# Retention and a mixture of experts in one kernel: another order of loads and operands in the opening, and weights fetched two rounds ahead at the switch of batches

## The chip, the cores and the metric

The kernel runs on one core of a Trainium2 chip. The metric is the device time of one execution in microseconds (us). Five engines work side by side, each through its own instructions in order: TensorE (PE, with its weight load PEld), VectorE (DVE), ScalarE (ACT), GpSimd (POOL) and SyncE (SP), which here only issues DMA transfers. They wait for each other by semaphores.

## The reference

Retention over q, k, v of 4 batches, 8 heads, 768 steps and 64 features, and its result as the input of four experts:

```python
for t in range(S):
    state = gamma[None, :, None, None] * state + np.einsum('bhd,bhe->bhde', k[:, :, t], v[:, :, t])
    y[:, :, t] = scale * np.einsum('bhd,bhde->bhe', q[:, :, t], state)
...
x = np.ascontiguousarray(attn_out.transpose(0, 2, 1, 3)).reshape(B * S, H * D)
...
p = domain_probs / (domain_probs.sum(-1, keepdims=True) + 1e-09)
for e in range(E):
    h = np.maximum(x @ w1[e], 0.0)
    out += p[:, e:e + 1] * (h @ w2[e])
```

x is 3072 x 512, w1 is 4 x 512 x 1024, w2 is 4 x 1024 x 512, all float32.

## The kernel before, in words

**Retention.** A batch is cut into 6 chunks of 128 steps. For each chunk `scores` (L131) multiplies q and k on PE and DVE applies the mask (`sp`, L142); `scale_v` (L125) scales v by powers of gamma on POOL; `state` (L144) adds k times v to the running state `yst` (DVE, L159), which `decay` (L161) has scaled down on POOL; `values` (L169) computes the cross term (q with the old state, L180) and the inner term (`sp` with v, L186) on PE, and DVE writes the result to `xr` (L195). Chunk c's values are issued after the scores of chunk c + 1.

**Experts.** Each batch passes 16 rounds, a round being 256 columns of one expert's hidden layer. The products are split in a Strassen-like way: seven pieces (numbered 1 to 7) of sums and differences of x and of w1 per round, in the order 1, 5, 6, 2, 7, 3, 4 (round 0: 1, 2, 5, 6, 7, 3, 4). Every operand exists as a high part, a copy to a rounded float (`x_hi`, `w1_hi`, `hi2`, on ACT), and a low part, the remainder (`x_lo`, `w1_lo`, `lo2`, a subtraction of two SBUF tiles on DVE or POOL). A piece (`p1`, L483) is then six matmuls into a PSUM bank. Some pieces are copied out by ACT (`u`, L414) and added by DVE to the next (L420). `hidden` (L427) makes the high and low part of the hidden values in batch 0; the second product (`p2`, L526) of round n - 1 is issued between the pieces of round n, and DVE adds it up in `acc` (L545).

x is combined chunk by chunk: `first_x(c, part)` (L325) makes, for chunk c, the operands 5 and 6 (part 0: DVE computes t1 and t2, ACT their high, DVE their low parts) or 7, 3 and 4 (part 1: two subtractions on POOL, then high and low parts). x's operands 1 and 2 need no combination. A piece needs its operand from all three chunks of the batch's first half, and that half is combined with the second half, so chunks 3 to 5 have to be there first.

`combine_w1` (four subtractions or additions of 128x256), `w1_hi`, `w1_lo` in two parts (128x768 as loaded, 128x1024 combined) make a round's w1 operands; `combine_w2` makes w2's second set in place, between `hi2`/`lo2` of the first (`w2h`, `w2l`) and of the second (`c2h`, `c2l`). In batch 0 all of them are stored to DRAM (`save_w1`, `save_w2`); the later batches fetch them from there, a piece at a time (`fetch_w1`, L310, into five buffers named `v`). From round 16 on `gated` (L449) makes the hidden operands (`b`, high `oh`, low `ol`), and puts each step in a list `soon` with the number of pieces that it waits; `pass_step` (L477) issues what is due. The output units (`unit`, L553) of rounds 16 and 17 begin in round 18.

**What sets the order.** The program is written out by hand: each engine gets its instructions in the order of the Python statements. `weights(n, k)` (L332) hangs the preparation of the next round's weights on the pieces of this one; the opening (L629 to L692) is a loop over the six chunks with such steps hung on chunk numbers. Transfers are issued by SP, and a few by ACT, in order; eight completion semaphores go round, so each waits until the one eight before it has landed. In the opening some chunks' q, k, v land in buffers that later hold weights, since those are free.

Of the kernel before, what the change touches and what calls it, by code (L numbers as in the profile page):

```python
# [24 lines left out]
NB0 = S // 128  # L25
# [25 lines left out]
def retention_moe(ctx: ExitStack, tc: tile.TileContext, qk, kv, w1, w2, probs, probt, cmask, cqs, cks, cys, out, out_t):  # L51
# [64 lines left out]
            (eng or nc.sync).dma_start(out=t, in_=qk[ci])  # L116
            raw_qk[ci] = t

    def load_kv(ci, pool=None, tag=None, eng=None):
        if ci < NCH:  # L120
            t = (pool or in_p).tile([128, 2, H, D], F32, tag=tag or "kv", name="kv", bufs=None if pool else 2)
            (eng or nc.sync).dma_start(out=t, in_=kv[ci])
            raw_kv[ci] = t

# [207 lines left out]
    def weights(n, k):  # L332

        m = n + 1
        if n == 0:
            if k == 0:
                first_x(2, 0)
                first_x(1, 1)
                first_x(2, 1)
                combine_w1(1, nc.gpsimd)  # L340
            elif k == 3:
                kept.pop("c11")()
                w1_hi(1, 0)
                w1_lo(1, 0, nc.vector)
                load_w1(2)
                w1_hi(1, 1)
                w1_lo(1, 1, nc.gpsimd)
            elif k == 4:
                save_w2(0, wt2, 0)
                combine_w2(0, nc.gpsimd)  # L350
            elif k == 5:
                hi2(0, wc2, "c2")
                save_w1(0)
            elif k == 6:
                lo2(0, wc2, nc.vector)
                load_w2(1)
                save_w1(1)
            return
        if k == 0:
            save_w2(n - 1, wc2, 4)  # L360
            if m < NRND:
                load_w1(m + 1)
                combine_w1(m, nc.gpsimd)
                w1_hi(m, 0)
        elif k == 1:
            hi2(n, wt2, "w2")
            if m < NRND:
                w1_lo(m, 0, nc.gpsimd)
        elif k == 2:
            lo2(n, wt2, nc.vector)  # L370
            if n == 2:
                gates()
        elif k == 3:
            save_w2(n, wt2, 0)
            combine_w2(n, nc.gpsimd)
            if m < NRND:
                w1_hi(m, 1)
        elif k == 4:
            hi2(n, wc2, "c2")
        elif k == 5:  # L380
            if m < NRND:
                w1_lo(m, 1, nc.gpsimd)
            lo2(n, wc2, nc.vector)
            load_w2(n + 1)
        elif k == 6 and m < NRND:
            save_w1(m)


    kept_g = keep_p.tile([NE, NTOK], F32, tag="kg", name="kg")

# [58 lines left out]
    def gated(n, key, src):  # L449

        f, j = key
        t = npool["b"].tile([128, HB], F32, tag="b", name="b")
        g = gate[n // RPE][:, HB * j:HB * j + HB]
        nc.vector.scalar_tensor_tensor(out=t, in0=src, scalar=0.0, in1=g, op0=ALU.max, op1=ALU.mult)  # L454
        hb[n, key] = t
        sub = lambda o, a, b: nc.gpsimd.tensor_tensor(out=o, in0=a, in1=b, op=ALU.subtract)  # L456
        if key in ((0, 0), (1, 1)):
            i = 1 if key == (0, 0) else 3
            soon.append((0, lambda: op_hi(n, i, t)))
            soon.append((1, lambda: op_lo(n, i)))  # L460
        elif key == (0, 1):
            b11, b22, b12 = hb[n, (0, 0)], hb[n, (1, 1)], t

            soon.append((1, lambda: (sub(b11, b12, b11), sub(b12, b22, b12), sub(b22, b22, b11))))
            soon.append((2, lambda: op_hi(n, 5, b11)))
            soon.append((2, lambda: op_lo(n, 5)))
            soon.append((3, lambda: (op_hi(n, 7, b12), op_hi(n, 6, b22))))
            soon.append((3, lambda: (op_lo(n, 7), op_lo(n, 6))))
        else:
            b22 = hb[n, (1, 1)]  # L470
            soon.append((1, lambda: op_hi(n, 2, t)))
            soon.append((2, lambda: op_lo(n, 2)))
            soon.append((3, lambda: sub(t, t, b22)))
            soon.append((4, lambda: op_hi(n, 4, t)))
            soon.append((5, lambda: op_lo(n, 4)))

    def pass_step():  # L477
        now = [f for t, f in soon if t == 0]
# [150 lines left out]
    with tc.manual_schedule():  # L629
        warm = u_p.tile([128, HB], F32, tag="u", name="warm", bufs=3)  # L630
        nc.vector.memset(warm, 0.0)
        load_qk(0)
        load_kv(0, eng=nc.scalar)
        nc.scalar.dma_start(out=ks, in_=cks)
        nc.scalar.dma_start(out=mask, in_=cmask)
        nc.scalar.dma_start(out=qs, in_=cqs)
        load_qk(1, v_p, "w2h")
        load_kv(1)
        nc.scalar.dma_start(out=ys, in_=cys)
        load_qk(2, v_p, "w2l")  # L640
        load_kv(2, w_p, "w1h")
        load_qk(3, w_p, "w1l")
        load_w1(0)
        nc.sync.dma_start(out=pr, in_=probs)
        nc.sync.dma_start(out=gr, in_=probt)
        load_w2(0)
        load_qk(4)
        load_kv(3)
        load_qk(5, v_p, "w2h")
        load_kv(5, v_p, "w2l")  # L650
        load_kv(4)
        load_w1(1)
        wps = ps_z.tile([128, 512], F32, tag="z", name="ps_w")
        for w in WARM:
            nc.tensor.matmul(wps[:, 0:w], lhsT=warm[:, 0:128], rhs=warm[:, 0:w], start=True, stop=True)
        for ci in range(NCHB):
            old = ci > 0
            scale_v(ci)
            scores(ci)
            if ci == 5:  # L660
                first_x(0, 1)
            if old:
                values(ci - 1, ci < NCHB - 1)
            else:
                state(ci)()
            if ci + 1 < NCHB:
                decay(ci + 1)
            if ci == 1:
                w1_hi(0, 0)
                combine_w1(0, nc.vector)  # L670
                w1_lo(0, 0, nc.vector)
            elif ci == 2:
                w1_hi(0, 1)
                w1_lo(0, 1, nc.vector)
                nc.vector.tensor_reduce(out=ptot, in_=pr, op=ALU.add, axis=mybir.AxisListType.X)
                nc.vector.tensor_scalar(out=ptot, in0=ptot, scalar1=1e-9, scalar2=None, op0=ALU.add)
                nc.vector.reciprocal(out=prec[:, :, 0], in_=ptot)
                nc.vector.tensor_tensor(out=pm, in0=pr, in1=prec.to_broadcast([128, NB0, NE]), op=ALU.mult)
# [12 lines left out]
        start[0] = False  # L691
        values(ci, False)  # L692

        steps = iter(())
        for n in range(NRND * B):
# [114 lines left out]
```

## Time and profile before

| | |
|---|---|
| median of 3 runs | 1091.43 us (1091.34 to 1093.07) |
| profiled execution, its own time | 1093.62 us |
| its span from first to last instruction | 1090.7 us |
| PE busy | 1050.8 us |
| DVE, ACT, POOL busy | 724.4, 378.3, 679.6 us |
| mean granted TensorE clock | 0.992 |

The profile is of one execution. Its page gives busy times, the chain of work that ended last and the costliest groups of instructions. Further views answer for a stretch of time: busy time by stretch with the granted clock, the list of who waited for whom, and a timeline of one engine, where a row has the start, the length, the engine, the line, the operation, out<-in and, in brackets, the idle time before it with its releaser. `L142` is line 142 of the kernel printed above.

### The profile page before, as it was taken

The page shows a single profiled execution, that of the slowest core. Times are in us where ns is not written, and L with a number is a line of the kernel's source. Part 1 is how long each engine was busy: PE and PEld are TensorE (multiplying, and loading weights), DVE is VectorE, ACT ScalarE, POOL GpSimd, SP SyncE. Part 2 cuts the span into 40 slices and gives each one's busy share as a digit, 9 for nine tenths or more (in the row PEclk, how much of TensorE's full clock was granted, in tenths as well). Part 3 has the DMA queues.
Part 4 walks back from the last instruction along what each step waited for, and adds up shares of the span by engine and source line. Part 5 has one row for each costly group of instructions (what it writes and reads, how often), then busy time and mean ns, then how long its engine had stood idle before and what let it go on. Part 6 is the DMA issues. An engine that isn't in the chain of part 4 may idle for free.

```text
span 1090.7 us, 18579 instructions
## 1 busy us (share of the span) xinstructions
PE 1050.8 (96%) x6696; PEld 993.4 (91%) x6696; DVE 724.4 (66%) x1214; ACT 378.3 (35%) x737; POOL 679.6 (62%) x645
## 2 busy tenths in 40 slices
PE   6689999999999999999999899999999899999996
PEld 5578888888878999999999899999999899999995
DVE  5857666676766476676688556667669546666665
ACT  2343433444443423223252432332233343333330
POOL 3566666666626656556579655656668865555557
PEclk9899999999999999999999999999999999999999
DMA  8479999999898888878786987877788788888875
GB/s 323 145 261 312 345 308 312 300 347 310 285 303 291 262 268 265 277 258 271 242 260 219 331 279 238 272 266 257 233 256 261 254 270 253 261 262 256 265 223 168
DMA packets 154603, 293.70 MB, mean 269 GB/s; under 512 B 12688, under 2 KB 77328, under 8 KB 154512
## 3 DMA queue, kind: packets, MB, share of 16 engines
q1 hardware_dynamic: 153792, 291.66, 81.9%
q8 instruction: 53, 0.87, 0.3%
q10 hardware_dynamic: 720, 0.86, 0.2%
q14 instruction: 38, 0.31, 0.1%
HBM read 223.22 MB, written 69.26 MB: 268 GB/s over the span
## 4 chain that ended last, share of the span: by engine, by line
PE 81%; DVE 7%; POOL 5%; DMA 3%; issue 2%; ACT 1%; SPq 0%; ACTq 0%; DVEq 0%; POOLq 0%
PE ps_u L563 28%; PE ps_x L502 22%; PE ps_o L537 11%; PE ps_z L502 11%; PE ps_y L502 5%; POOL b L456 2%; POOL sum L578 2%; PE ps_s L139 2%; PE ps_v L186 2%; DVE xl L240 2%; DVE ol L447 1%; POOL ol L447 1%; PE ps_v L180 1%; DMA w2r<-in_w 1%; DMA v<-k 1%
## 5 line engine op out<-in xcount | busy, mean ns | idle before, releaser
L563 PE MATMUL ps_u<-oh,v 128*128 128x384 f32 x1344 | 395.5, 336 | 8.5 <-DVE sum L420 8.5
L456 POOL TENSOR_TENSOR b<-b 128x384 f32<-128x384 f32 x192 | 206.7, 1076 | 179.0 <-DVE b L454 147.5
L563 PEld LDWEIGHTS ps_u<-oh,v 128*128 128x128 f32 x1344 | 247.8, 188 | 12.2 <-DVE sum L420 12.0
L447 POOL TENSOR_TENSOR ol<-b,oh 128x384 fp32r<-128x384 f32 x192 | 207.8, 1094 | 81.1 <-ACT oh L442 43.5
L420 DVE TENSOR_TENSOR sum<-ps_u,sum 128x384 f32<-128x384 f32 x294 | 161.7, 550 | 136.4 <-PE ps_u L563 129.0
L442 ACT ACTIVATE oh<-b 128x384 fp32r<-128x384 f32 x336 | 163.1, 520 | 214.5 <-POOL b L456 123.8
L502 PE MATMUL ps_x<-xh,v 128*128 128x384 f32 x768 | 227.2, 336 | 1.3 <-ACT u L414 1.3
L563 PE MATMUL ps_u<-ol,v 128*128 128x384 f32 x672 | 225.0, 335 | 1.3 <-POOL ol L447 1.3
L414 ACT ACTIVATE u<-ps_x 128x384 f32<-128x384 f32 x128 | 62.6, 489 | 238.5 <-PE ps_x L502 238.4
L502 PEld LDWEIGHTS ps_x<-xh,v 128*128 128x128 f32 x768 | 141.4, 188 | 3.4 <-ACT u L414 1.6
L447 DVE TENSOR_TENSOR ol<-b,oh 128x384 fp32r<-128x384 f32 x144 | 127.9, 888 | 22.2 <-ACT oh L442 22.1
L502 PE MATMUL ps_x<-xl,v 128*128 128x384 f32 x384 | 128.4, 334 | 0.0
L563 PEld LDWEIGHTS ps_u<-ol,v 128*128 128x128 f32 x672 | 126.3, 188 | 1.7 <-POOL ol L447 1.7
L502 PE MATMUL ps_z<-xh,v 128*128 128x384 f32 x384 | 115.0, 340 | 2.4 <-DMA v<-k 2.4
L545 DVE SCALAR_TENSOR_TENSOR acc<-ps_o,pm,acc 128x512 f32<-128x512 f32 x90 | 67.0, 745 | 54.9 <-PE ps_o L537 54.9
L537 PE MATMUL ps_o<-w2l,hh 128*128 128x512 f32 x192 | 76.6, 399 | 0.0
L537 PE MATMUL ps_o<-w2h,hh 128*128 128x512 f32 x192 | 76.5, 398 | 0.2
L537 PE MATMUL ps_o<-w2h,hl 128*128 128x512 f32 x192 | 76.5, 398 | 0.0
L502 PEld LDWEIGHTS ps_z<-xh,v 128*128 128x128 f32 x384 | 71.6, 190 | 3.8 <-DVE c2l L290 2.7
L502 PEld LDWEIGHTS ps_x<-xl,v 128*128 128x128 f32 x384 | 72.1, 188 | 0.1
L502 PE MATMUL ps_z<-xl,v 128*128 128x384 f32 x192 | 64.8, 338 | 0.0
L420 DVE TENSOR_TENSOR ps_y<-ps_y,u 128x384 f32<-128x384 f32 x64 | 36.0, 563 | 33.6 <-PE ps_y L502 33.6
(109 smaller groups left out, 1630.5 us busy)
## 6 DMA issues: line engine op xcount, KB each, us to landing
v<-k SPq DMA_DIRECT2D x336, 256.0 KB, 3.8
v<-k SPq DMA_DIRECT2D x168, 512.0 KB, 4.5
k<-w1h SPq DMA_DIRECT2D x16, 896.0 KB, 6.3
k<-w1l SPq DMA_DIRECT2D x16, 896.0 KB, 8.4
qk<-in_qk SPq DMA_DIRECT2D x24, 512.0 KB, 5.5
kv<-in_kv SPq DMA_DIRECT2D x23, 512.0 KB, 5.8
w1r<-in_w SPq DMA_DIRECT2D x16, 512.0 KB, 7.9
w2r<-in_w SPq DMA_DIRECT2D x16, 512.0 KB, 4.3
```

The source lines that it names most:

```text
L139: nc.tensor.matmul(ps[r][:, p, :], lhsT=a[rows, 1, p, :], rhs=a[rows, 0, p, :], start=True, stop=True)
L186: nc.tensor.matmul(ps[r][64 * k:64 * k + 64, half, :], lhsT=v[:, 1, h, :], rhs=sp[:, h, :], start=(c == 0 and half == 0), stop=True, skip_ ...
L240: eng.tensor_tensor(out=lo, in0=x_part(b, i, o), in1=hi.bitcast(F32), op=ALU.subtract)
L414: nc.scalar.activation(out=t, in_=ps, func=ACTF.Copy)
L420: nc.vector.tensor_tensor(out=o, in0=ps, in1=u, op=ALU.add)
L442: nc.scalar.activation(out=hi, in_=t, func=ACTF.Copy)
L447: eng.tensor_tensor(out=lo, in0=t, in1=hi.bitcast(F32), op=ALU.subtract)
L456: sub = lambda o, a, b: nc.gpsimd.tensor_tensor(out=o, in0=a, in1=b, op=ALU.subtract)
L502: nc.tensor.matmul(ps, lhsT=lhsT[:, cs], rhs=rhs[:, kt, :], start=(fresh and m == 0), stop=(m == 5), skip_group_check=True,)
L537: nc.tensor.matmul(ps, lhsT=a[:, ts], rhs=b[:, fs, :], start=(m == 0), stop=(m == 5))
L545: nc.vector.scalar_tensor_tensor(out=acc[nt], in0=ps, scalar=sc, in1=acc[nt], op0=ALU.mult, op1=ALU.add)
L563: nc.tensor.matmul(ps, lhsT=w[:, r, l, ds], rhs=o, start=(m == 0), stop=(m == 5))
```

## The change

- **Loads.** mask and ks become the first two of ACT's transfers, ahead of v and k of chunk 0; ys goes ahead of qs. On SP round 0's w1 goes ahead of chunk 3's q; chunk 3's and 4's k and v land in the buffers of `c2h` and `c2l` and so wait for no one; probs move to the end; round 2's w1 is loaded in the opening.
- **Scaling.** v of chunk c + 1 is scaled after the state of chunk c and ahead of the decay for c + 1; before, v of a chunk was scaled at the chunk's own start.
- **Operands.** Round 0's `combine_w1`, both `w1_lo`, `lo2` of w2 and `x_lo` of operand 1 move from DVE to POOL. The four steps that normalise probs move out of the loop into `first_gates`, at piece 2 of round 0. `first_x(0, 1)` moves from the last chunk to round 0; `first_x(1, 0)` moves behind the last values. `combine_w2(0)` moves from piece 4 to piece 2, ahead of `w1_lo(1, 1)` on POOL; `hi2`, `lo2` of the second set and the next load of w2 move one piece up.
- **Switch.** The first four pieces of round 16's w1 are fetched at the start of round 14 and no longer in round 15; in round 16 `gated` doubles every wait in `soon`.

```diff
@@ weights, n == 0
             if k == 0:
                 first_x(2, 0)
+                first_x(0, 1)
                 first_x(1, 1)
                 first_x(2, 1)
                 combine_w1(1, nc.gpsimd)
+            elif k == 2:
+                first_gates()
+                save_w2(0, wt2, 0)
+                combine_w2(0, nc.gpsimd)
             elif k == 3:
                 kept.pop("c11")()
                 w1_hi(1, 0)
                 w1_lo(1, 0, nc.vector)
-                load_w1(2)
                 w1_hi(1, 1)
                 w1_lo(1, 1, nc.gpsimd)
             elif k == 4:
-                save_w2(0, wt2, 0)
-                combine_w2(0, nc.gpsimd)
-            elif k == 5:
                 hi2(0, wc2, "c2")
                 save_w1(0)
-            elif k == 6:
+            elif k == 5:
                 lo2(0, wc2, nc.vector)
                 load_w2(1)
+            elif k == 6:
                 save_w1(1)
@@ gated
+        slow = 2 if n == NRND else 1
+        later = lambda w, what: soon.append((w * slow, what))
...
-            soon.append((0, lambda: op_hi(n, i, t)))
-            soon.append((1, lambda: op_lo(n, i)))
+            later(0, lambda: op_hi(n, i, t))
+            later(1, lambda: op_lo(n, i))
...
@@ the opening
+        nc.scalar.dma_start(out=mask, in_=cmask)
+        nc.scalar.dma_start(out=ks, in_=cks)
         load_qk(0)
         load_kv(0, eng=nc.scalar)
-        nc.scalar.dma_start(out=ks, in_=cks)
-        nc.scalar.dma_start(out=mask, in_=cmask)
+        nc.scalar.dma_start(out=ys, in_=cys)
         nc.scalar.dma_start(out=qs, in_=cqs)
         load_qk(1, v_p, "w2h")
         load_kv(1)
-        nc.scalar.dma_start(out=ys, in_=cys)
         load_qk(2, v_p, "w2l")
         load_kv(2, w_p, "w1h")
+        load_w1(0)
         load_qk(3, w_p, "w1l")
-        load_w1(0)
+        load_kv(3, v_p, "c2h", 1)
+        load_qk(4)
+        load_kv(4, v_p, "c2l", 1)
+        load_qk(5, v_p, "w2h")
+        load_kv(5, v_p, "w2l")
+        load_w2(0)
+        load_w1(1)
         nc.sync.dma_start(out=pr, in_=probs)
         nc.sync.dma_start(out=gr, in_=probt)
-        load_w2(0)
-        load_qk(4)
-        load_kv(3)
-        load_qk(5, v_p, "w2h")
-        load_kv(5, v_p, "w2l")
-        load_kv(4)
-        load_w1(1)
...
+        scale_v(0)
         for ci in range(NCHB):
             old = ci > 0
-            scale_v(ci)
             scores(ci)
             if ci == 5:
-                first_x(0, 1)
+                first_x(0, 0)
             if old:
                 values(ci - 1, ci < NCHB - 1)
             else:
                 state(ci)()
             if ci + 1 < NCHB:
+                scale_v(ci + 1)
                 decay(ci + 1)
             if ci == 1:
                 w1_hi(0, 0)
-                combine_w1(0, nc.vector)
-                w1_lo(0, 0, nc.vector)
+                combine_w1(0, nc.gpsimd)
             elif ci == 2:
                 w1_hi(0, 1)
-                w1_lo(0, 1, nc.vector)
...
+                w1_lo(0, 0, nc.gpsimd)
             elif ci == 3:
-                hi2(0, wt2, "w2")
-                lo2(0, wt2, nc.vector)
                 for i in (1, 2):
                     x_hi(0, i)
-                    x_lo(0, i)
+                w1_lo(0, 1, nc.gpsimd)
+                x_lo(0, 1, eng=nc.gpsimd)
             elif ci == 4:
-                first_x(0, 0)
+                x_lo(0, 2)
+                hi2(0, wt2, "w2")
+                load_w1(2)
                 load_qk(6)
                 load_kv(6)
-            elif ci == 5:
-                first_x(1, 0)
         start[0] = False
         values(ci, False)
+        first_x(1, 0)
+        lo2(0, wt2, nc.gpsimd)
@@ the rounds
-                fetch_w1(t + 4)
+                if t == 7 * (NRND - 2):
+                    for x in range(4):
+                        fetch_w1(7 * NRND + x)
+                if t >= 7 * NRND:
+                    fetch_w1(t + 4)
```

Two places in the order of the built programs. First POOL in the opening, from the scaling of v of chunk 2; `kv` is the tile whose half v is scaled, `yst_115` and `yst_116` the two state tiles, `s` the combined w1, `w1l` its low part. Before:

```order
L127 TENSOR_TENSOR kv<-kv,ks 128x512
L165 TENSOR_TENSOR yst_115<-yst_115,ys 128x256
L127 TENSOR_TENSOR kv<-kv,ks 128x512
L165 TENSOR_TENSOR yst_116<-yst_116,ys 128x256
L127 TENSOR_TENSOR kv<-kv,ks 128x512
L165 TENSOR_TENSOR yst_115<-yst_115,ys 128x256
L127 TENSOR_TENSOR kv<-kv,ks 128x512
L212 TENSOR_TENSOR xr<-xr 128x2x128
```

The same place now, from just behind the decay for chunk 2:

```order
L265 TENSOR_TENSOR s<-w1r 128x256
L266 TENSOR_TENSOR s<-s,w1r 128x256
L267 TENSOR_TENSOR s<-w1r,s 128x256
L268 TENSOR_TENSOR s<-w1r 128x256
L127 TENSOR_TENSOR kv<-kv,ks 128x512
L165 TENSOR_TENSOR yst_115<-yst_115,ys 128x256
L282 TENSOR_TENSOR w1l<-w1r,w1h 128x768
L127 TENSOR_TENSOR kv<-kv,ks 128x512
L165 TENSOR_TENSOR yst_116<-yst_116,ys 128x256
L282 TENSOR_TENSOR w1l<-s,w1h 128x1024
L240 TENSOR_TENSOR xl<-xr,xh 128x768
L127 TENSOR_TENSOR kv<-kv,ks 128x512
```

The scaling and decays of chunks 3 to 5 now have w1's four combinations, its two low parts and one low part of x between them; the last decay and w2's low part (128x1024) follow.

Then ACT at the switch, in round 17: `u` is a copied piece that PE's next piece in that bank waits for, `oh` a high part of hidden values. Before:

```order
L414 ACTIVATE u<-ps_x 128x384
L442 ACTIVATE oh<-b 128x384 x2
L414 ACTIVATE u<-ps_z 128x384
L442 ACTIVATE oh<-b 128x384 x2
L414 ACTIVATE u<-ps_x 128x384
L442 ACTIVATE oh<-b 128x384 x3
```

The same place now:

```order
L422 ACTIVATE u<-ps_x 128x384
L422 ACTIVATE u<-ps_z 128x384
L450 ACTIVATE oh<-b 128x384
L422 ACTIVATE u<-ps_x 128x384
L450 ACTIVATE oh<-b 128x384 x5
```

Three of the four `oh` that stood between round 17's first and third copy now stand behind the third.

More of the change, by code (lines that the diff above doesn't have):

```diff
@@ L117, in load_qk, with load_kv @@
             raw_qk[ci] = t
-    def load_kv(ci, pool=None, tag=None, eng=None):
+    def load_kv(ci, pool=None, tag=None, bufs=None, eng=None):
         if ci < NCH:
-            t = (pool or in_p).tile([128, 2, H, D], F32, tag=tag or "kv", name="kv", bufs=None if pool else 2)
+            t = (pool or in_p).tile([128, 2, H, D], F32, tag=tag or "kv", name="kv", bufs=bufs if pool else 2)
             (eng or nc.sync).dma_start(out=t, in_=kv[ci])
@@ L386, in weights, with first_gates @@
             save_w1(m)
+    def first_gates():
+        nc.vector.tensor_reduce(out=ptot, in_=pr, op=ALU.add, axis=mybir.AxisListType.X)
+        nc.vector.tensor_scalar(out=ptot, in0=ptot, scalar1=1e-9, scalar2=None, op0=ALU.add)
+        nc.vector.reciprocal(out=prec[:, :, 0], in_=ptot)
+        nc.vector.tensor_tensor(out=pm, in0=pr, in1=prec.to_broadcast([128, NB0, NE]), op=ALU.mult)
     kept_g = keep_p.tile([NE, NTOK], F32, tag="kg", name="kg")
@@ L458, in gated @@
             i = 1 if key == (0, 0) else 3
-            soon.append((0, lambda: op_hi(n, i, t)))
-            soon.append((1, lambda: op_lo(n, i)))
+            later(0, lambda: op_hi(n, i, t))
+            later(1, lambda: op_lo(n, i))
         elif key == (0, 1):
             b11, b22, b12 = hb[n, (0, 0)], hb[n, (1, 1)], t
[L464 to L468, printed above, removed]
+            later(1, lambda: (sub(b11, b12, b11), sub(b12, b22, b12), sub(b22, b22, b11)))
+            later(2, lambda: op_hi(n, 5, b11))
+            later(2, lambda: op_lo(n, 5))
+            later(3, lambda: (op_hi(n, 7, b12), op_hi(n, 6, b22)))
+            later(3, lambda: (op_lo(n, 7), op_lo(n, 6)))
         else:
             b22 = hb[n, (1, 1)]
[L471 to L475, printed above, removed]
+            later(1, lambda: op_hi(n, 2, t))
+            later(2, lambda: op_lo(n, 2))
+            later(3, lambda: sub(t, t, b22))
+            later(4, lambda: op_hi(n, 4, t))
+            later(5, lambda: op_lo(n, 4))
     def pass_step():
@@ L669, in retention_moe @@
                 w1_hi(0, 0)
-                combine_w1(0, nc.vector)
-                w1_lo(0, 0, nc.vector)
+                combine_w1(0, nc.gpsimd)
             elif ci == 2:
                 w1_hi(0, 1)
-                w1_lo(0, 1, nc.vector)
[L675 to L678, printed above, removed]
+                w1_lo(0, 0, nc.gpsimd)
             elif ci == 3:
-                hi2(0, wt2, "w2")
-                lo2(0, wt2, nc.vector)
                 for i in (1, 2):
                     x_hi(0, i)
-                    x_lo(0, i)
+                w1_lo(0, 1, nc.gpsimd)
+                x_lo(0, 1, eng=nc.gpsimd)
             elif ci == 4:
-                first_x(0, 0)
+                x_lo(0, 2)
+                hi2(0, wt2, "w2")
+                load_w1(2)
                 load_qk(6)
                 load_kv(6)
-            elif ci == 5:
-                first_x(1, 0)
         start[0] = False
         values(ci, False)
+        first_x(1, 0)
+        lo2(0, wt2, nc.gpsimd)
         steps = iter(())
```

## The prediction

> **What bounds the kernel now.** I read the page first: TensorE (PE) is busy for 96% of the span, so all there is to gain are the few places where it is not. The table by stretches shows where those are. Its columns are busy time of PE, weight load, DVE, ACT and POOL, then the granted TensorE clock, the DMA share and GB/s.
>
> ```profile
> PE 1050.8 (96%) x6696; PEld 993.4 (91%) x6696; DVE 724.4 (66%) x1214; ACT 378.3 (35%) x737; POOL 679.6 (62%) x645
> 10.00:20.00 10.00, 8.53 (x154) 6.90 (x156) 8.17 (x17) 2.85 (x3) 3.41 (x4) 1.00 1.03 397
> 20.00:30.00 10.00, 5.13 (x100) 4.22 (x98) 9.90 (x16) 1.58 (x2) 5.63 (x4) 1.00 0.67 238
> 30.00:40.00 10.00, 7.10 (x81) 5.66 (x78) 9.91 (x20) 2.81 (x7) 5.35 (x6) 0.76 1.00 351
> 40.00:50.00 10.00, 7.50 (x33) 6.30 (x32) 9.21 (x16) 5.83 (x14) 5.24 (x7) 0.90 0.00 0
> 60.00:70.00 10.00, 8.02 (x33) 6.74 (x32) 5.00 (x9) 3.58 (x6) 5.62 (x6) 0.83 0.96 324
> 300.00:400.00 100.00, 96.17 (x568) 90.21 (x567) 60.00 (x98) 40.28 (x83) 51.29 (x49) 0.98 0.87 287
> ```
>
> From 20 to 50 us DVE is full (9.9, 9.9 and 9.2 us of 10) and PE is not: there DVE sets the pace. The clock falls as well, to 0.76, 0.90 and 0.83. The next hole that the change reaches is at the switch from batch 0 to batch 1. The list of PE's waits for 0 to 80 us and for 290 to 345 us (total, times, longest) names who is late:
>
> ```profile
> PE ps_v L153 <- POOL kv L127: 6.0, 4, 2.7
> PE ps_x L502 <- ACT u L414: 4.1, 3, 2.0
> PE ps_v L180 <- DVE sp L142: 2.5, 1, 2.5
> PE ps_z L502 <- DMA v<-k: 2.4, 1, 2.4
> PE ps_x L502 <- ACT u L414: 1.3, 1, 1.3
> ```
>
> The largest entry, v scaled by POOL too late, looks like the gain of this change. It isn't the term to count: what matters is when PE last waits in the opening. Those rows (start, length, engine, line) are these:
>
> ```profile
> 47.63 0.55 DVE L420 TENSOR_TENSOR ps_y<-ps_y,u 128x384 f32<-128x384 f32 x1
> 53.66 0.44 PE L502 MATMUL ps_z<-xh,w1h 128*128 128x384 f32 x1 [0.35 <-DVE hl L435]
> 56.03 1.06 ACT L286 ACTIVATE c2h<-w2r 128x1024 fp32r<-128x1024 f32 x1 [3.02 <-POOL w2r L298]
> 59.44 4.00 DMA w2r<-in_w
> 64.49 0.48 ACT u L414
> 65.02 0.44 PE L502 MATMUL ps_x<-xh,w1h 128*128 128x384 f32 x1 [1.98 <-ACT u L414]
> ```
>
> ```profile
> 75.42 1.04 PE ps_x L502 x6
> 77.50 1.39 PE ps_o L537 x6
> ```
>
> The last two, from the chain that ended last, are a piece and an output of TensorE at full clock. Call 47.63 us C: DVE starts round 0's first addition of hidden values. Call 65.02 us T: PE starts round 1's fifth piece. After T it waits for nothing up to round 16, so whatever T moves, the end moves.
>
> **Loads and scaling, up to C.** In the new order mask and ks go first and v is scaled a chunk ahead. That takes away the first wait for ks and the four waits for kv, and I count it at nothing by itself, because the six chunks now queue behind POOL. POOL receives five jobs that DVE had. Rows: the landing of w1, then POOL's decay and scaling (alone, and beside DVE), one addition, and the two sizes of low parts:
>
> ```profile
> 8.38 6.77 DMA w1r<-in_w
> 11.15 0.61 POOL L165 TENSOR_TENSOR yst<-yst,ys 128x256 f32<-128x256 f32 x1 [1.97 <-DVE yst L158]
> 11.72 1.04 POOL L127 TENSOR_TENSOR kv<-kv,ks 128x512 f32<-128x512 f32 x1
> 25.63 1.46 POOL L165 TENSOR_TENSOR yst<-yst,ys 128x256 f32<-128x256 f32 x1 [2.38 <-DVE yst L159]
> 27.05 1.75 POOL L127 TENSOR_TENSOR kv<-kv,ks 128x512 f32<-128x512 f32 x1
> 56.76 0.72 POOL L266 TENSOR_TENSOR s<-s,w1r 128x256 f32<-128x256 f32 x1
> 59.94 1.84 POOL L282 TENSOR_TENSOR w1l<-w1r,w1h 128x768 fp32r<-128x768 f32 x1
> 69.04 2.40 POOL L282 TENSOR_TENSOR w1l<-s,w1h 128x1024 fp32r<-128x1024 f32 x1
> 31.16 1.09 PE L186 MATMUL ps_v<-sp,kv 128*64 128x128 f32 x16
> 36.64 1.97 PE L186 MATMUL ps_v<-sp,kv 128*64 128x128 f32 x16
> 38.54 0.69 PE L502 MATMUL ps_x<-xh,w1h 128*128 128x384 f32 x1
> ```
>
> w1 landed at 15.15 us; one load of 512 KB fewer is ahead of it, 1.3 us at the 397 GB/s of 10 to 20 us, so 13.8. From there POOL has, in order: four combinations (4 x 0.8 with the gaps, 3.2), scaling and decay three times (3 x 1.65, 5.0), w1l 1.84 and 2.40, and xl of 128x768, taken as the w1l of that size, 1.84. Sum 14.3: it ends at 28.1 if nothing disturbs it. With the three pairs at their long lengths (1.46 and 1.75) it is 32.8. The long ones stood beside DVE's additions of two SBUF tiles, of which five are left in this time, so I take a value nearer the short end, 29.5. The last decay is what PE's last cross term waits for, so the attention ends 0.7 and 1.09 us later, V = 31.3 (32.8 with the 1.97 of the half clock). Before, it ended at 38.6: seven us won.
>
> They are spent at once. Between V and C DVE had ten additions on 128x256 pieces; now it has seventeen, and then the gates' four small steps:
>
> ```profile
> 21.70 0.17 DVE L675 TENSOR_REDUCE ptot<-pr 128x6 f32<-128x24 f32 x1
> 22.54 0.76 DVE L678 TENSOR_TENSOR pm<-pr,prec 128x24 f32<-128x24 f32 x1
> 36.73 0.41 DVE L240 TENSOR_TENSOR xl<-t,xh 128x256 fp32r<-128x256 f32 x1
> 43.22 0.92 POOL L265 TENSOR_TENSOR s<-w1r 128x256 f32<-128x256 f32 x1
> 43.47 1.83 DVE L240 TENSOR_TENSOR xl<-xr,xh 128x256 fp32r<-128x256 f32 x2
> ```
>
> One takes 0.41 us alone and 0.92 while POOL works on such a piece, which itself takes 0.92 in place of 0.72. POOL, after w2's low part (29.5 + 2.40 = 31.9), has fourteen such pieces without a wait: six of x, four of w1, four of w2; 14 x 0.92 = 12.9, until 44.8. DVE starts at V + 0.7 = 32.0, does fourteen of its own in that time, three more alone (1.2, to 46.0) and the gates (21.70 to 23.30, 1.6): C = 47.6, where it was. Bounds: all seventeen alone gives 32.0 + 7.0 + 1.6 = 40.6; all contended from V = 35.8 gives 53.7. I take 47.6, because POOL's fourteen pieces are really there.
>
> [...]
>
> **From C to T.** DVE, ACT and PE go hand to hand from C to 53.66, and the order there is kept: 6.0 us again. After it round 0's w2 combinations are the difference. They stood behind w1l on POOL, and c2h on ACT waited for them until 56.03, so the next w2 was fetched only at 59.44 and u came late for T. Now they run before w1l, in the fourteen pieces above. c2h follows at C + 4, c2l by C + 7.2, w2 lands 4.0 later, then 1.06 on ACT and u 0.48: C + 12.8. PE needs from 53.66 on three pieces of 1.04 and three outputs of 1.39, so T = C + 6.0 + 7.3 = C + 13.3 = 60.9; PE is later than u by 0.5. T was C + 17.4: 4.1 us. The new order has a wait to watch: c2h now stands ahead of round 0's last two hidden copies and of u on ACT, and would hold them if POOL's w2 pieces ended after C + 4; by the sum above they end at 44.8, seven us before. On SP round 2's w1 now waits for POOL's first w1l, with chunk 6 and the first saves behind it, none of them needed before round 1: nothing.
>
> The clock: 0.83 over 60 to 70 is 1.7 us of PE work lost just behind T, after its waits. Without them I count 1.7 us back.
>
> **The switch to batch 1.** Four weight pieces of round 16 are fetched two rounds earlier. Rows at the place:
>
> ```profile
> 318.21 0.41 PE L502 MATMUL ps_z<-xh,v 128*128 128x384 f32 x1 [2.41 <-DMA v<-k]
> 318.76 0.74 DVE L545 SCALAR_TENSOR_TENSOR acc<-ps_o,pm,acc 128x512 f32<-128x512 f32 x1
> 320.38 0.63 PE L537 MATMUL ps_o<-w2l,hh 128*128 128x512 f32 x1
> 322.28 0.39 PE L537 MATMUL ps_o<-w2h,hh 128*128 128x512 f32 x1
> ```
>
> The wait of 2.41 goes, and the slow matmuls behind it (0.63 for 0.39). What is late next is DVE's accumulation, through at 319.5: round 16's second output needs its bank. It began at 322.28, so 2.8 us come back and not the 3.8 of wait and clock. The extra fetches, 4 x 256 KB in round 14, meet a DMA share like the 0.87 of 300 to 400 us, but that round loads no w1 (512 KB), and SP's next load is the w2 that DVE releases at the round's end: nothing. The doubled delays in round 16 move `oh` behind the copy `u` on ACT, and the 1.3 us wait goes. Their later place in rounds 17 and 18 is hidden under steps of a piece and a unit, 2 us each; without that cover it would cost up to the 1.3 again.
>
> **Sum.** 4.1 + 1.7 + 2.8 + 1.3 = 9.9 us (C itself moves by nothing). The profiled execution would go from 1093.62 to 1083.7; it lies 2.2 us over the median of the three runs, 1091.43, whose spread of 1.73 is that of one half-clock stretch. Set against the median: 1081.5.
>
> **The rivals.**
> Shorter block: POOL's pieces wait for DVE's (the second pair of x needs t of its own chunk), so fewer collide, C = 43: 1077. For it: the 0.41 at 36.73 stood where POOL waited for DVE's t. Against: the four of w1 and the four of w2 wait for nothing there. Chance 0.17.
>
> The clock: PE idles some 4 us before the last decay and works 5 pieces between V and C, less than in 30 to 40 us where 0.76 was granted; two half-clock stretches then end in the PE-bound work behind C and cost 2 x 1.7: 1084.9. Chance 0.15. [...]
>
> The switch gives nothing, since the delayed operands collide with DVE's and POOL's work of round 17: 1085.6. Chance 0.07.
>
> The queue: all of POOL's moved work at long lengths, C = 53.7, with one more half-clock stretch: 1081.5 + 6.1 + 1.7 = 1089.3, no change. Chance 0.08.
>
> Slower: POOL becomes the bound of the opening. The place is the last decay, behind w1l and xl in POOL's queue, and PE's last cross term behind it. The price is one us for each that C comes later; it loses from C = 57.5 on, measurably from 59.7. That needs V near 42, moved pieces at about twice their length, as decay already took 1.46 for 0.61. At C = 62 it is 1095.9. Against it: those long lengths had DVE's SBUF work beside them, which is what leaves. Chance 0.06.
>
> **How the numbers follow.** My forecast has 0.47, its own range 1079 to 1084.5 (C from 45 to 50.5). A median is told from no change here at about 0.2%, 2.2 us, so below 1089.2 is faster: 0.47 + 0.17 + 0.15 + 0.07 = 0.86; the queue is 0.08 for no change, the last 0.06 for slower. The range 1075.5 to 1088 leaves out the queue, the slower case and the far end of the short block.
>
> **What would show it.** Right: the last attention values end at 30 to 33 us with PE's wait named POOL yst; DVE and POOL both full from 32 to 45; the first ps_y addition near 47; c2h waits no longer for POOL; T near 61 at full clock; no wait for DMA v in round 16, but one of about 1 us for DVE acc; no wait for ACT u in round 17. Wrong: C well off 47.6 (the lengths of pieces side by side), a low clock after T, a POOL decay before the last cross term later than 35, or a wait for w2 or v in rounds 14 to 18.

## The result, and the profile after

| | before | changed |
|---|---|---|
| median | 1091.38 us (4 runs, 1088.97 to 1093.07) | 1083.58 us (4 runs, 1082.23 to 1088.06) |
| profiled execution, its own time | 1093.62 us | 1088.06 us |
| its span | 1090.7 us | 1086.0 us |
| mean granted clock | 0.992 | 0.987 |

The ratio of the two sets of runs is 0.9938 (95% interval 0.9909 to 0.9967), which is 6.8 us faster, 3.6 to 9.9; the two medians, of four runs each, lie 7.8 us apart. The forecast was 1081.5 and the range 1075.5 to 1088.0. The profiled execution of the changed kernel is the slowest of its four, so its trace shows less of the gain than the median does.

The table by stretches (columns as before: PE, weight load, DVE, ACT, POOL, granted clock, DMA share, GB/s), of the changed kernel:

```profile
10.00:20.00 10.00, 9.85 (x164) 8.84 (x166) 5.83 (x13) 0.98 (x2) 6.37 (x10) 0.83 1.03 408
20.00:30.00 10.00, 7.64 (x144) 6.25 (x142) 7.96 (x15) 3.57 (x5) 10.00 (x8) 1.00 0.88 292
30.00:40.00 10.00, 6.01 (x46) 4.77 (x47) 9.88 (x15) 3.38 (x10) 8.85 (x9) 0.83 0.63 209
40.00:50.00 10.00, 5.68 (x22) 5.10 (x23) 9.34 (x16) 3.68 (x11) 6.94 (x9) 0.75 0.21 69
50.00:60.00 10.00, 8.75 (x37) 7.83 (x36) 5.65 (x9) 5.39 (x9) 7.95 (x6) 0.74 0.23 73
60.00:70.00 10.00, 10.00 (x61) 8.68 (x61) 7.50 (x12) 4.93 (x7) 7.05 (x7) 1.00 1.07 377
```

From 20 to 30 us it is now POOL that is full, and PE gets 7.64 us in place of 5.13. From 30 to 50 DVE is full as before (9.88 and 9.34), so that block was moved and not removed. The low clock stands ahead of T (0.75 and 0.74) and no longer behind it (1.00 from 60 to 70, before 0.83); there is also one from 10 to 20 us (0.83), which before did not have (1.00).

PE's waits of the changed kernel (total, times, longest), first from 0 to 80 us, then from 270 to 345:

```profile
PE ps_v L180 <- POOL yst L165: 3.9, 1, 3.9
PE ps_x L512 <- DVE xl L240: 3.4, 1, 3.4
PE ps_z L512 <- ACT xh L236: 2.0, 1, 2.0
...
PE ps_x L512 <- DVE ps_c L428: 1.3, 1, 1.3
...
PE ps_o L547 <- DVE acc L555: 1.3, 2, 1.1
PE ps_z L512 <- DMA v<-k: 1.1, 1, 1.1
PE ps_x L512 <- ACT u L422: 0.7, 1, 0.7
```

The four waits for scaled v (6.0 us) are gone from the first list, and one of 3.9 us for POOL's last decay has come. In the second the 2.4 us for v in round 16 and the 1.3 us for u in round 17 are gone; DVE's accumulation is next late in round 16, as the prediction said, but there is also a new wait for v, in round 18. The 0.7 us for u in this list lie in round 15, at 304 us; the second profile of this kernel has no such wait there. The rows of the milestones (the last decay, V, DVE's first piece behind the last eviction, the first of the gates, C, c2h, T, and the second output of round 16):

```profile
30.70 0.79 POOL L165 TENSOR_TENSOR yst<-yst,ys 128x256 f32<-128x256 f32 x1
32.61 1.97 PE L186 MATMUL ps_v<-sp,kv 128*64 128x128 f32 x16
35.52 0.41 DVE L212 TENSOR_TENSOR t<-xr 128x256 f32<-128x256 f32 x1
47.88 0.16 DVE L392 TENSOR_REDUCE ptot<-pr 128x6 f32<-128x24 f32 x1
48.61 0.56 DVE L428 TENSOR_TENSOR ps_y<-ps_y,u 128x384 f32<-128x384 f32 x1
52.31 1.05 ACT L286 ACTIVATE c2h<-w2r 128x1024 fp32r<-128x1024 f32 x1
62.94 0.33 PE L512 MATMUL ps_x<-xh,w1h 128*128 128x384 f32 x1
316.96 0.50 PE L547 MATMUL ps_o<-w2h,hh 128*128 128x512 f32 x1 [1.07 <-DVE acc L555]
```

V, the end of the attention, is 34.6 us (forecast 31.3, before 38.6), C 48.61 (47.6, before 47.63), T 62.94 (60.9, before 65.02). c2h starts without a wait (no bracket); T has none either.

### The profile page after: what moved, and what is told of

The parts are those of the page before. It is cut to its first block, busy times and chain, and to the rows that moved or that the text cites. A ratio compares the mean times of both kernels' runs of the same rounds, so it can differ in the third digit from the quotient of the medians.

```text
span 1086.0 us, 18584 instructions
## 1 busy us (share of the span) xinstructions
PE 1052.4 (97%) x6696; PEld 996.0 (92%) x6696; DVE 721.9 (66%) x1206; ACT 378.2 (35%) x737; POOL 689.9 (64%) x653
## 4 chain that ended last, share of the span: by engine, by line
PE 83%; DVE 7%; POOL 4%; issue 2%; DMA 2%; ACT 1%; SPq 0%; ACTq 0%; DVEq 0%; POOLq 0%
PE ps_u L573 28%; PE ps_x L512 22%; PE ps_o L547 11%; PE ps_z L512 11%; PE ps_y L512 5%; PE ps_v L186 2%; PE ps_s L139 2%; DVE xl L240 2%; POOL sum L588 2%; POOL b L466 1%; DVE ol L455 1%; PE ps_v L180 1%; POOL ol L455 1%; DVE b L464 1%; PE ps_v L153 1%
```

## The experiments

In what follows a half-clock stretch is a stretch for which the trace records a granted clock of 0.5.

Theory: the sum of the prediction, which is 5.8 us from the opening (4.1 at T, 1.7 of clock behind it) and 4.1 from the switch (2.8 by the early fetch, 1.3 by the doubled delay). Rivals: the switch gives little; POOL's queue sets C; the half clock sets T. The median of before was 1091.2, 1091.6, 1090.5 and 1093.2 us on the four occasions, 9 to 22 runs each; ratios are to before on the same chip.

**The switch and the opening apart.** First the early fetch alone, in the kernel before:

```diff
-                fetch_w1(t + 4)
+                if t == 7 * (NRND - 2):
+                    for x in range(4):
+                        fetch_w1(7 * NRND + x)
+                if t >= 7 * NRND:
+                    fetch_w1(t + 4)
```

> The kernel before with only the early fetch of the four pieces of round 16; the opening and the delays are before's. The prediction's sum: 2.8 us faster than before; in the trace the wait DMA v<-k of 2.4 us in round 16 is gone and one of about 1 us for DVE acc stands there. Rival (the two terms of the switch overlap: without the doubled delay the time comes back one round later as a wait of PE for ACT u or DVE b): under 1.5 us faster.

Measured: 1090.51 us, ratio 0.9990 (0.9977 to 1.0002), so 1.1 us faster, from 2.5 faster to 0.2 slower. The 2.8 us are outside. Yet the trace shows what was forecast: no wait for v, and this row for the output behind it, 3.1 us earlier than in the first profile of before (322.28):

```profile
319.19 0.50 PE L537 MATMUL ps_o<-w2h,hh 128*128 128x512 f32 x1 [1.05 <-DVE acc L545]
```

So the profile of before came under suspicion. It was taken once more:

> The kernel before once more, for a second profile. [...]

PE in round 16 of that second profile:

```profile
317.93 0.41 PE L502 MATMUL ps_z<-xh,v 128*128 128x384 f32 x1 [1.41 <-DMA v<-k]
...
319.07 0.40 PE L537 MATMUL ps_o<-w2h,hh 128*128 128x512 f32 x1
...
320.47 0.40 PE L537 MATMUL ps_o<-w2h,hh 128*128 128x512 f32 x1
```

The wait is 1.41 us and not 2.41, and the outputs run at 0.40 us each and not 0.63: there is no half-clock stretch. From the first piece of round 16 to its second output it takes 7.69 us in the first profile of before, 5.15 in the second, 5.16 in the next kernel (which fetches late too), and 4.92 to 4.96 in all eleven traces with the early fetch. The fetch is worth 2.7 us against the first profile and 0.2 against the others.

Next the changed kernel without the two edits of the switch (both parts of this), and without the doubled delay alone (the first part):

```diff
-        slow = 2 if n == NRND else 1
+        slow = 1
...
-                if t == 7 * (NRND - 2):
-                    for x in range(4):
-                        fetch_w1(7 * NRND + x)
-                if t >= 7 * NRND:
-                    fetch_w1(t + 4)
+                fetch_w1(t + 4)
```

> The changed kernel with the switch to batch 1 as before (no early fetch, no doubled delay): the opening alone. The prediction's sum: 4.1 + 1.7 = 5.8 us faster than before. Reading of the two traces: 2.1 us at T, 1.7 us behind it, and 0.9 us given back in round 15, so 2.9 to 3.7 us. Rival (everything measured comes from the switch, and the opening only moves its waits): within 1 us of before.

> The changed kernel without the doubled delay of the operand steps in round 16. The prediction's sum: 1.3 us slower than the changed kernel, with the 1.3 us wait of PE for ACT u in round 17 back. Rival (what the delay gains is given back by a wait for DVE b and one for DMA v in rounds 17 and 18, since PE then meets the chain of fetches sooner): no difference over 0.5 us, and the wait for DMA v of 1.1 us in round 18 smaller or gone.

Measured: the opening alone 1086.52 us, ratio 0.9953 (0.9937 to 0.9970), 5.1 us faster (3.3 to 6.9). The forecast of 5.8 lies inside, and so, at the end, does the reading of the traces. Without the delay 1085.53 us, ratio 0.9952 (0.9932 to 0.9971); the changed kernel, run again, had this:

> The changed kernel once more, unchanged, for its median on this chip and for a second drawing of the half-clock stretches. Expected: 6.8 us under before (ratio 0.9938 so far), the same named waits, T at 62 to 63; which half-clock stretches there are should differ by one or two from the first profile (two or three in a row between 44 and 55 us).

It gave 1084.59 us, ratio 0.9935 (0.9919 to 0.9951), 7.1 us faster. The intervals with and without the delay overlap, so medians do not settle 1.3 us. The traces say more. This is PE's wait in round 17 without the delay, and below it all that PE waited for from 312 to 352 us in the kernel with the delay, run again:

```profile
PE ps_x L512 <- ACT u L422: 1.0, 1, 1.0
```

```profile
PE ps_o L547 <- DVE acc L555: 1.0, 1, 1.0
PE ps_z L512 <- DMA v<-k: 0.5, 1, 0.5
```

The delay does take the wait for u away. But from the second output of round 16 to the second piece of round 18 it takes 24.57 to 24.92 us in the five traces without the delay (mean 24.72) and 23.12 to 24.96 in the nine with it (mean 24.25), since seven of the nine wait for v or for DVE's `b` in rounds 17 and 18 instead, 0.5 to 1.1 us. Some 0.5 us stays of 1.3. These waits are what PE meets next when it comes sooner; what makes that v late was not tried.

**From C to T.** The second half of round 0's w2 back at the later pieces:

```diff
             elif k == 2:
                 first_gates()
-                save_w2(0, wt2, 0)
-                combine_w2(0, nc.gpsimd)
...
             elif k == 4:
-                hi2(0, wc2, "c2")
-                save_w1(0)
+                save_w2(0, wt2, 0)
+                combine_w2(0, nc.gpsimd)
             elif k == 5:
-                lo2(0, wc2, nc.vector)
-                load_w2(1)
+                hi2(0, wc2, "c2")
+                save_w1(0)
             elif k == 6:
+                lo2(0, wc2, nc.vector)
+                load_w2(1)
                 save_w1(1)
```

> The changed kernel with round 0's second-half w2 (its combinations on POOL, its copy on ACT, its low part on DVE) back at the later pieces, where before had them. The prediction's step from C to T: c2h waits for POOL again, the next w2 lands 4 us later, T is 4.1 us later (C + 17.4), and the kernel 4 us slower than the changed one, nearly all that the opening gained. Rival (POOL's four pieces in the block before C cost as much there as they save behind it): C comes 2 us earlier or more, and the time is within 1.5 us of the changed kernel.

Measured: 1087.28 us, ratio 0.9967 (0.9953 to 0.9980), 3.6 us faster than before, half of what the changed kernel has. Rows of its c2h and T, and its stretch from 60 to 70 us:

```profile
54.82 1.06 ACT L286 ACTIVATE c2h<-w2r 128x1024 fp32r<-128x1024 f32 x1 [2.95 <-POOL w2r L298]
```

```profile
63.70 0.44 PE L512 MATMUL ps_x<-xh,w1h 128*128 128x384 f32 x1 [1.86 <-ACT u L422]
```

```profile
60.00:70.00 10.00, 8.14 (x32) 6.81 (x31) 5.35 (x9) 4.73 (x7) 5.78 (x6) 0.83 1.03 335
```

Both sides were right on their own part. C came at 46.48 us, 2.1 earlier, four pieces of POOL at 0.5 each, as the rival said, but its 1.5 us for the time were exceeded (3.5). T came at C + 17.2, where the prediction's step has C + 17.4 for this order. c2h waits 2.95 us for POOL again, PE 1.86 for u, and behind that wait the half clock is back (0.83). So T itself is only 0.8 us later than in the first profile of the changed kernel, and 0.7 earlier than in the second (64.40); the clock behind T costs 1.2 us more (the thirteen matmuls behind it take 3.85 us for 2.61). Where the rest of the 3.5 us lost lies, these traces do not show.

**Does POOL's queue set C?** The last scaling and decay ahead of two long low parts (which also change places):

```diff
-                w1_lo(0, 1, nc.gpsimd)
-                x_lo(0, 1, eng=nc.gpsimd)
             elif ci == 4:
+                x_lo(0, 1, eng=nc.gpsimd)
+                w1_lo(0, 1, nc.gpsimd)
```

> The changed kernel with POOL's last scaling and decay ahead of the two low parts (128x768 of x, 128x1024 of w1) that stood before them. The queue theory (PE's 3.9 us for the last decay set the attention's end, and DVE's block starts there): the decay ends near 26.7 instead of 31.5, the attention's end V comes at 30 instead of 34.5, C follows by 3 to 4 us (44.6 to 45.6), T by as much, and the kernel is 3 to 4 us faster than the changed one. Rival (DVE's block waits for POOL's six pieces of x, which come no earlier): V earlier as said, C by less than 1.5 us, the time by less than 1.5 us.

Measured: 1085.39 us, ratio 0.9946 (0.9932 to 0.9959). V came at 29.3 us, 5.3 earlier, and C at 49.65, one us later. PE's first wait of its list, then POOL, then DVE:

```profile
PE ps_y L512 <- DVE xr L195: 5.6, 1, 5.6
```

```profile
29.13 2.54 POOL L282 TENSOR_TENSOR w1l<-s,w1h 128x1024 fp32r<-128x1024 f32 x1
31.64 2.52 POOL L290 TENSOR_TENSOR w2l<-w2r,w2h 128x1024 fp32r<-128x1024 f32 x1
```

```profile
29.48 2.47 DVE L212 TENSOR_TENSOR t<-xr,t 128x256 f32<-128x256 f32 x1
31.88 3.42 DVE L240 TENSOR_TENSOR xl<-t,xh 128x256 fp32r<-128x256 f32 x2
35.22 1.41 DVE L195 TENSOR_TENSOR xr<-ps_v,qs 128x256 f32<-128x256 f32 x4
```

The wait for the decay turned into a wait of 5.6 us for DVE's eviction, because DVE's pieces of 128x256, 0.41 us alone, took much longer beside POOL's instructions of 2.5: one took 2.47, and two together took 3.42 where two alone take 0.75. The queue theory falls. The rival had the right size but named the wrong cause: POOL's six pieces of x were not what DVE waited for. T came at 65.13, 2.2 us later than in the first profile of the changed kernel, because C was one us later and C to T took 15.48; the experiment on the clock below shows why it was that long.

The other way round, the two w1 low parts back on DVE:

```diff
-                w1_lo(0, 0, nc.gpsimd)
+                w1_lo(0, 0, nc.vector)
...
-                w1_lo(0, 1, nc.gpsimd)
+                w1_lo(0, 1, nc.vector)
```

> The changed kernel with round 0's two w1 low parts (128x768 and 128x1024) back on DVE, where it waits for PE between the chunks of the attention. If the queue on POOL sets C: POOL's last decay ends 2 to 4 us earlier, the attention's end V comes at 31 to 32.5 and C 2 us earlier, the kernel 2 us faster than the changed one. If DVE is the bound from 28 us on and every piece on POOL beside it costs it about half a piece: DVE is through with the long pieces earlier, but has 2.0 us more of its own, C within 1 us of 48.6 and the time within 1 us of the changed kernel. If DVE's own 2.0 us lengthen the chunks of the attention: C 2 us later, the time 2 us longer.

Measured: 1083.70 us, ratio 0.9933 (0.9918 to 0.9947), no different from the changed kernel. V 31.8, C 48.93. DVE's block, from the eviction of the last values to C, takes 14.4 us here (34.52 to 48.93), in the changed kernel (34.19 to 48.61) and in the kernel with the decay first (35.22 to 49.65). Whatever V gains, DVE spends: the second theory.

**Is POOL's help in the block worth anything?** Its eight combinations on DVE:

```diff
-                combine_w1(1, nc.gpsimd)
+                combine_w1(1, nc.vector)
...
-                combine_w2(0, nc.gpsimd)
+                combine_w2(0, nc.vector)
```

> The changed kernel with the eight 128x256 combinations of round 1's w1 and round 0's w2 on DVE instead of POOL, in the block before C. The prediction's price (a DVE piece takes 0.92 us beside a POOL piece and 0.41 alone, so POOL's eight cost DVE 4.1 us, and eight more of its own cost 8 x 0.45 = 3.6): the DVE pieces that had them beside them take 0.41 each, C is where it was or up to 0.5 us earlier (48.1 to 48.6), the time within 1 us of the changed kernel. Rival (the two engines work side by side, and what POOL takes over is saved): C 3.5 us later, near 52, and the kernel 3.5 us slower.

Measured: 1084.69 us, ratio 0.9942 (0.9926 to 0.9957). C came at 48.64, with eight instructions more on DVE. The same place in the block, the changed kernel first:

```profile
43.22 1.80 DVE L240 TENSOR_TENSOR xl<-xr,xh 128x256 fp32r<-128x256 f32 x2
44.95 0.94 DVE L240 TENSOR_TENSOR xl<-t,xh 128x256 fp32r<-128x256 f32 x1
```

```profile
42.58 0.75 DVE L240 TENSOR_TENSOR xl<-xr,xh 128x256 fp32r<-128x256 f32 x2
43.25 0.41 DVE L240 TENSOR_TENSOR xl<-t,xh 128x256 fp32r<-128x256 f32 x1
...
44.60 0.41 DVE L265 TENSOR_TENSOR s<-w1r 128x256 f32<-128x256 f32 x1
```

Without POOL beside it a piece takes 0.41 us in place of 0.94, and DVE does POOL's pieces in 0.41 to 0.43 each. The block is 13.5 us long (35.18 to 48.64), one us shorter than with POOL's help. The rival's 3.5 us do not exist.

**The clock ahead of T.** Matmuls whose results nobody reads, ahead of four pieces of round 0:

```diff
+BUSY = {5: 10, 6: 4, 7: 17, 4: 6}
...
+                if n == 0 and i in BUSY:
+                    busy(BUSY[i], ps_o.tile([128, 512], F32, tag="o", name="ps_w")[:, 0:HB])
                 p1(n, i)
```

> The changed kernel with 37 matmuls more in round 0 whose results nobody reads, 6 to 17 of them ahead of each of four pieces, in the time in which PE waits there. Clock theory (the 1.0 us by which C to T came out longer than 13.3 is the half clock of 45 to 55 us, earned by PE's waits from 37 to 47): no half-clock stretch between 44 and 55, C to T near 13.3, T 1 us earlier or more, the kernel about 1 us faster than the changed one. Rival (ACT and DVE hand the pieces on, and PE's clock is beside the path there): the clock full and T, C to T and the time the same within 0.5 us.

Measured: 1085.03 us, ratio 0.9935 (0.9921 to 0.9949). Its stretches:

```profile
40.00:50.00 10.00, 9.10 (x51) 8.47 (x50) 9.34 (x16) 3.71 (x11) 6.93 (x9) 1.00 0.20 66
50.00:60.00 10.00, 7.75 (x40) 6.89 (x40) 5.82 (x10) 5.84 (x10) 7.97 (x6) 1.00 0.31 93
```

The half clock is gone (1.00 for 0.75 and 0.74), C is at 48.60 as before, T at 62.06, so C to T 13.46 and the clock theory holds in the trace. The other traces whose program is the same from C on say where the clock matters:

| kernel | C | half clock ends | past C | C to T |
|---|---|---|---|---|
| matmuls that nobody reads | 48.60 | 37.6 | ahead of C | 13.46 |
| w1's low parts on DVE | 48.93 | 50.6 | 1.7 | 13.45 |
| opening alone | 48.40 | 51.0 | 2.6 | 13.48 |
| changed, first profile | 48.61 | 55.2 | 6.6 | 14.33 |
| without the delay | 48.47 | 55.7 | 7.2 | 14.59 |
| changed, second profile | 49.59 | 57.2 | 7.6 | 14.81 |
| decay first | 49.65 | 58.8 | 9.2 | 15.48 |

Half clock up to C + 2.6 cost nothing (C to T is 13.45 to 13.48 in the first three rows): PE waits for DVE there, as the rival said. In the first three rows PE still waits 0.3 us for DVE's `hl` at C + 6; in the other four that wait is gone, since the slow matmuls have made PE the late one. My estimate from the table is that each us that the half clock reaches past about C + 5 costs half a us (9.2 - 5 is 4.2, and 15.48 is 2.0 over 13.46). In the kernel with the combinations on DVE it reaches 8.5 us past C, and C to T is 15.16 there. The median of the kernel with the added matmuls did not move, though: one us is inside the interval of 1.5 either way.

**A better version?** The combinations on DVE as above, three steps off the way from C to T, and in the second of the two kernels matmuls as in the last one (`BUSY = {5: 10, 6: 3, 4: 16}`):

```diff
             elif k == 2:
-                first_gates()
                 save_w2(0, wt2, 0)
...
             elif k == 3:
-                kept.pop("c11")()
                 w1_hi(1, 0)
-                w1_lo(1, 0, nc.vector)
                 w1_hi(1, 1)
+                gap[0, (0, 0)] = first_gates
+                gap[0, (1, 1)] = lambda: w1_lo(1, 0, nc.vector)
+                kept.pop("c11")()
                 w1_lo(1, 1, nc.gpsimd)
@@ hidden, behind the high part
+        gap.pop((n, key), lambda: None)()
```

> The kernel with the eight combinations on DVE, and with work of DVE and ACT moved off the way from C to T: the gates' four small steps (0.74 us) stand behind the first ps_y addition, where DVE waits 0.56 us for ACT; round 1's two high copies of w1 stand on ACT ahead of C; its first low part (0.96 us) stands behind the second hidden addition. If that way is DVE's and ACT's hand-over, as the prediction had it: C 0.7 us earlier (47.9), PE's wait for ps_c 0.9 us shorter, T at 60.5 to 61.8, and the kernel 1 to 2 us faster than the changed one. Rival (the fetch of the next w2 sets T, at C + 12.8 whatever PE does): only the 0.7 us of the gates, and no measurable difference.

> The same with 29 matmuls more in round 0 whose results nobody reads, in the time in which PE waits ahead of three pieces, so that the clock stays full. Clock theory: no half-clock stretch between 40 and 60 us, T another 0.5 to 1 us earlier than without them when that one has a stretch there, the kernel 2 to 3 us faster than the changed one. Rival (as the first trial with such matmuls: the stretch goes and the median does not): the same median as without them within 0.7 us.

Measured: 1086.62 us, ratio 0.9944 (0.9927 to 0.9961), and with the matmuls 1084.13 us, 0.9931 (0.9911 to 0.9950). Neither is better than the changed kernel. The first one's T, 61.08 us, is in the range that was expected, but for another reason: its attention ended at 33.0, 1.6 us earlier than in the first profile of the changed kernel. Up to there the two programs are the same. What differs is the clock: the first profile of the changed kernel has half clock from 10.8 to 14.3 us and this trace has none ahead of 29.5. POOL's rows around that stretch, the changed kernel's two first, then this one's:

```profile
12.04 1.04 POOL L127 TENSOR_TENSOR kv<-kv,ks 128x512 f32<-128x512 f32 x1
16.23 0.61 POOL L165 TENSOR_TENSOR yst<-yst,ys 128x256 f32<-128x256 f32 x1 [3.15 <-DVE yst L159]
```

```profile
12.03 1.05 POOL L127 TENSOR_TENSOR kv<-kv,ks 128x512 f32<-128x512 f32 x1
14.62 0.61 POOL L165 TENSOR_TENSOR yst<-yst,ys 128x256 f32<-128x256 f32 x1 [1.54 <-DVE yst L159]
```

The 1.6 us arise there, where PE is busy nearly all the time (9.85 of 10 us in the changed kernel); they are still there at the last decay (31.49 and 29.90) and at the start of DVE's block (34.19 and 32.59). Nine of the eleven traces with the changed opening have such an early stretch, between 9 and 17 us; this one and the next kernel's have none. PE's wait for ps_c, expected to be 0.9 us shorter, is 6.4 us for 1.3, while its 3.4 us for xl are gone. And DVE lost 2.1 us of its block again at one row. POOL, then DVE:

```profile
44.85 2.34 POOL L282 TENSOR_TENSOR w1l<-s,w1h 128x1024 fp32r<-128x1024 f32 x1 [6.06 <-ACT w1h L277]
```

```profile
44.97 2.50 DVE L298 TENSOR_TENSOR w2r<-w2r 128x256 f32<-128x256 f32 x1
47.39 0.55 DVE L428 TENSOR_TENSOR ps_y<-ps_y,u 128x384 f32<-128x384 f32 x1
```

The earlier high copy let POOL's low part start at 44.85 us and no longer at 51.45, behind C, and DVE's last combination, 0.42 us alone, took 2.50 beside it. The second one, where no half clock was expected between 40 and 60 us, has it from 49.6 to 53.0, behind a wait of PE of 3.39 us that the added matmuls did not fill; its T, 60.87, is 0.2 us earlier and not 0.5 to 1. The intervals of the two ratios overlap, so the medians do not tell these two kernels apart.

## Why the prediction was right, and where not

The forecast of 1081.5 us came within 2.1 us of the median, and part of that is luck. It stood for 9.9 us; the terms that the traces confirm make about 4, and the medians 6.8 to 7.8. What follows takes the steps one by one.

**Right: the bound of the opening.** That V's seven us would be spent at once by DVE and POOL in the block before C was the step that mattered. V moved by 4.0 and C by one us the other way. The price behind it, 0.92 for a contended piece, is shown by the combinations on DVE. The sum inside was off by parts that nearly cancel, so that C came within one us of the forecast is luck: DVE's pieces and the gates took 13.1 us and not 15.6 (the gates 0.7 and not 1.6), but they began at 35.5 and not at 32.0. V, 34.6, lies outside the bounds of 31.3 to 32.8: the last decay ended at 31.5 and not at 29.5, and the last terms of the attention ran at the half clock (1.97 for 1.09). The early half-clock stretch is what the step left out of V: in the two traces without it the last decay ends at 29.9 and 29.8, nearly as forecast, and V is 33.0 and 32.8, at the upper bound. And one term was missing: DVE's four first pieces of x stood beside POOL's long instructions; the prediction put POOL's pieces of 128x256 into the block and let the long ones pass. The kernel with the decay first shows that this term alone is enough: V at 29.3 did not bring C forward.

**Right: C to T.** Forecast C + 13.3, measured 13.45 to 13.48 where the half clock ends by C + 2.6, 14.3 to 15.5 where it ends at C + 6.6 to C + 9.2; with the old order C + 17.2 for 17.4. c2h does not wait, as said. The step left out that the half clock moves to just ahead of T, where it costs up to 2.0 us (15.48 for 13.46; 0.9 and 1.35 in the two profiles of the changed kernel).

**Right: the clock behind T.** All three traces with the opening of before have a half-clock stretch just behind T, and there the thirteen matmuls behind it take 4.0 to 4.2 us; in the four with the changed opening they take 2.6. So the 1.7 is 1.5. At T itself the mean is 65.0 before and 63.1 after, 1.9 and not 4.1 us.

**Wrong: the switch.** "2.8 us come back" took the wait of 2.41 us and the slow matmuls from one execution as if every execution had them. The second profile has 1.41 and full clock, and the early fetch is worth 0.2 us there, 1.1 in the median. The step that named DVE's accumulation as next late was right, and it is the reason: that wait of 1.1 us is nearly as long as the ordinary wait for v. "Their later place in rounds 17 and 18 is hidden" failed too, by the new waits that leave 0.5 of 1.3; a wait for v in rounds 14 to 18 was listed as a sign of a wrong forecast, and it came.

**The rivals.** "The switch gives nothing" was nearest to what the switch does, and had 0.07. The clock rival's stretches are there, ending in the PE-bound work behind C (at C + 6.6 and C + 7.6), but by the estimate from the table only what reaches past C + 5 costs: 0.9 and 1.35 us in the two profiles of the changed kernel and not 2 x 1.7. The queue's mechanism is there as a wait of 3.9 us and decides nothing. The shorter block did not come: C was later.

**What stays open.** The terms as the traces show them, 1.9 + 1.5 at the opening and 0.2 + 0.5 at the switch, make 4.1 us; the medians say 6.8 and 7.1 (down to 3.6 and 5.3). Both profiled executions of the changed kernel are the slowest of their samples (1088.06 of 1082.23 to 1088.06, and 1087.54 of 1082.67 to 1087.54), so a typical execution must be shorter somewhere. The three unprofiled ones of the first four have a mean clock of 0.989 to 0.991 for 0.987, which suggests fewer half-clock stretches: one of 3.4 us lowers the mean over 1086 us by 0.0016, so 0.003 is about two of them. The two that the traces price are the early one (1.6 us up to V) and what reaches past C + 5 (0.9 to 1.35 us). None of the fast executions of the changed kernel was seen in a trace, so this is an estimate.

## What to carry to other kernels

Before a wait and the slow matmuls behind it are priced from one profile, take a second one: here 2.5 of the 2.7 us that the first profile showed for a term were that execution's own. Before work on two SBUF tiles moves from a full DVE to POOL, measure what DVE's own pieces take beside it: here they took 0.94 us for 0.41, and the block was 14.4 us long with eight pieces on POOL and 13.5 with them on DVE. An addition of DVE to PSUM took 0.56 us with POOL beside it and without, so such a place, or one where DVE waits, is the one to try. And when a late step is brought forward, look first at what stands in the queue of the engine that takes its result: the decay came 4 us earlier, and DVE was not there to use it.

## What the runs showed of the hardware

**Two engines on SBUF.** In two places a DVE piece of 128x256 on two SBUF tiles that started beside a long POOL instruction lasted until 0.3 us after that one ended: in the kernel with the combinations on DVE and steps off the way, 0.42 us became 2.50 beside 2.34 (end at 47.47 and 47.19), and in the kernel with the decay first 0.43 became 2.47 beside 2.54 (31.95 and 31.67). Where both had small pieces back to back, in the changed kernel, each piece of DVE took 0.94 us and not the sum of 1.13 (0.41 on DVE and 0.72 on POOL, each alone). That is still more than DVE needs for both pieces, 0.41 and 0.43: eight pieces moved from POOL to DVE made the block one us shorter (13.5 for 14.4). A DVE instruction that adds to PSUM was not held up: the addition to ps_z at 52.92 us of the changed kernel took 0.56 us beside POOL's w1l from 51.45 to 53.82, as long as the one at 48.61 with nothing on POOL.

**Half-clock stretches.** Every half-clock stretch in the middle of the fourteen traces is 3.4, 6.8 or 10.2 us long, and they lie differently from one profile to the next: in the two profiles of the changed kernel the stretches of the opening are 10.8 to 14.3, 31.3 to 34.7 and 45.0 to 55.2 us, and 9.5 to 16.3, 33.4 to 36.8, 40.2 to 43.6 and 47.0 to 57.2. Such a stretch cost time only where PE was the path: up to 1.6 us for the early one, nothing between C and C + 2.6. A wait of 2.4 us had such a stretch behind it in one trace; waits of 1.0 to 1.4 us at the same place had none in thirteen.
